# Packed attention with routed experts on Trainium2: the expert guess from VectorE's row sums, and one run of routing products over six PSUM banks

## The chip, the cores and the metric

One core of one Trainium2 chip runs the whole program in one launch. The metric is the device time of one execution in microseconds (us), and lower is better. The profile and the trace come from one profiled execution on the chip.

## What is computed

There are 8 batches of 8 heads, 576 tokens and head size 64. In each batch and head a set of 32 packed queries `p` attends over keys and values, which gives 32 packed rows. Each token's query then attends over these 32 rows, which are both its keys and its values. The 8 heads' results stand beside each other as a token row of 512 numbers, and a layer of 8 experts follows: cosine logits against 8 expert embeddings pick one expert for the token and weight its output.

```
p_packed = sm_attn(p, k, v)                  # softmax(p k^T / 8) v, 32 rows per head
x = sm_attn(q, p_packed, p_packed)           # tokens as rows of 512
xn, en = x / (|x| + 1e-6), emb / (|emb| + 1e-6)
logits = xn @ en.T / tau                     # 8 experts
e = argmax(logits); gate = softmax(logits)[e]
out = gate * (relu(x @ w1[e]) @ w2[e])       # w1: 512x1024, w2: 1024x512
```

## The kernel before, in words

Everything is float32; the large products of the expert layer are split into high and low parts of the type `fp32r` and take three products each. The order of every engine's work is written out by hand: TensorE, VectorE, ScalarE and GpSimd each run their instructions in the order in which the Python generators emit them, and semaphores alone hold one back. The expert layer of batch b, `ffn` (line 953), is the frame: it yields 56 times, after each group of its matmuls, and at each yield the driver (lines 1497 to 1517) calls `step_att` once, which emits one step of `att_main` (line 1119), the attention and routing of batch b+1. For batches 2 to 7 this order is the same each time. For batch 1 the steps come from the string list `PLAN` during batch 0's expert layer.

The steps of `ffn`: 16 times `hidden` (L1004, products against G, the first layer's weights already multiplied by the packed rows), 8 steps of L1039 (the last 64 tokens' second layer), and four chunks of 128 tokens (c = 0 to 3) with 8 steps of three L1057 matmuls each. In the last chunk `w1_rows` of the next batch (L934 on TensorE, L946 on ScalarE, L947 on VectorE, which make the next G) starts as soon as that batch's `route` has finished.

PSUM has eight banks, all given out: pool `ps` has three single banks named `pf` (the expert layer's), pool `pb` two double banks named `pt`, pool `pc` one single bank named `pu`. The order around the change:

- `att1` (line 528): `pair_turn` (L501) turns the packed rows `ppx` through TensorE, VectorE copies them to `x.T` (L568), and two steps later `row_logits` (L512: four matmuls of 8 columns) multiplies them with the embeddings `enT`; `logits_out` (L521, VectorE) puts the 8 results beside each packed row in `ppx`. The generator `queries` turns one pair of heads' queries on VectorE each time it is called (`flip`, L291); `query_scores` (L270, TensorE) needs all four turned pairs.
- `guess` (line 619): a matmul of the row logits with `itaus` (1/tau everywhere, L629) sums the logits over the packed rows; the largest of the 8 sums is the expert whose weights are loaded for the whole batch (L635 to L640 on VectorE, then DMAs from GpSimd's queue).
- `route` (line 757): for each of five chunks of tokens, two groups g of four heads and two halves of the partitions, one product (L766) of 64 rows, 128 tokens and 136 columns: 128 of values, 8 of logits. `sums` squares and adds the values on ScalarE (L778, with the accumulator read behind it) and adds the logits on VectorE (L781). Batches 1 to 7 take the chunks in two runs: chunks 0 and 1 in both `pt` tiles, and after their sums chunks 2, 3 and 4. The last chunk is computed over 128 tokens, of which the upper 64 count.
- `TURNS` (line 1080) says what each of eleven steps at the end of a batch's attention emits: `r` a step of `route`, `f` a turned pair of the next batch's keys.
- After `route`, the next batch's `quarter_banks` takes both `pt` tiles and sets their edges (L319, L320 on VectorE), and `quarter_scores` (L331) writes into them.

Of the kernel before, what the change touches and what calls it, by code (L numbers as in the profile page):

```python
# [17 lines left out]
P = 128  # L18
# [9 lines left out]
def kernel(  # L28
# [91 lines left out]

    itau = cp.tile([P, 1], F32, name="itau")
    fold = cp.tile([P, 32], F32, name="fold")
    itaus = cp.tile([P, 64], F32, name="itaus")
    enT = cp.tile([P, NPR, E], F32, name="enT")

    def embeddings():
# [41 lines left out]
                pt[:, pr * E : (pr + 1) * E], en_sb[:, pr * P : (pr + 1) * P], ident[:E, :E]  # L168
            )
        yield  # L170
        nc.scalar.copy(enT.rearrange("a b c -> a (b c)"), pt[:, : NPR * E])

    class Batch:
        def __init__(self):
# [65 lines left out]
    def rows(c):  # L240
        return P if c < 4 else 64
# [11 lines left out]
    def idle(n):  # L253
        for _ in range(n):
            yield
# [253 lines left out]
    def row_logits(x, pt, gs=range(NG)):  # L509
        for g in gs:  # L510
            for pr in range(2):
# [5 lines left out]
                    stop=True,  # L517
                )

    def logits_out(x, pt):  # L520
        nc.vector.tensor_copy(x.ppx[:, :, 2 * D :], pt[:, : NG * E].rearrange("p (g e) -> p g e", g=NG))  # L521

# [5 lines left out]
    def att1(x, nat, queries=None, other=None):  # L528

        def pack(queries, other):  # L530
            pack_tiles(x)
            if not x.s1:
                quarter_banks(x)
            quarter_scores(x)
            yield
            for g in range(NG):
                quarter_max(x, g)
            yield
            yield from whole_max(x)
# [24 lines left out]
            yield  # L564
            pu = pc.tile([P, 512], F32, name="pu", tag="pu")
            for g in range(NG):
                pair_turn(x, g, pu)
            nc.vector.tensor_copy(x.T, pu[:, 0 : NG * P])  # L568
            yield from idle(2)
            pt = pc.tile([P, 512], F32, name="pu", tag="pu")  # L570
            row_logits(x, pt)
            yield
            logits_out(x, pt)
            next(queries)
            yield

        def pack_slowly():
            pack_tiles(x)
# [20 lines left out]
            yield  # L599
            pt = pc.tile([P, 512], F32, name="pu", tag="pu")  # L600
            row_logits(x, pt)
            logits_out(x, pt)
            yield

        if x.halves:
# [13 lines left out]
    def guess(x, late=0, engine=mybir.EngineType.Pool, total=None):  # L619
# [5 lines left out]
                    pt[:1, :E], total[:, n : n + 1], enT[:, n], start=(n == 0), stop=(n == NPR - 1)  # L625
                )
        else:
            for g in range(NG):
                nc.tensor.matmul(  # L629
                    pt[:64, :E], itaus, x.ppx[:, g, 2 * D :], start=(g == 0), stop=(g == NG - 1)  # L630
                )
        yield
        m8 = sm.tile([1, 8], F32, name="m8", tag="m8", bufs=1)
        idx = sm.tile([1, 8], U32, name="idx", tag="idx", bufs=1)
# [5 lines left out]
        nc.vector.tensor_scalar(  # L640
            out=x.sel, in0=ecol[:1], scalar1=gi, scalar2=None, op0=ALU.is_equal
        )
        yield from idle(late)
        x.e = nc.values_load(
            idx[0:1, 0:1], engines=[engine], min_val=0, max_val=E - 1,
# [109 lines left out]


    def route(x):
        lg = sm.tile([P, NC5, E], F32, name="lg", tag="lg")
        ss = sm.tile([P, NC5], F32, name="ss", tag="ss")
        nc.gpsimd.memset(lg[:64, 4:5, :], 0.0)  # L760
        nc.gpsimd.memset(ss[:64, 4:5], 1.0)
        def product(c, g, to):
            n = min(c * P, S - P)
            for half in range(2):
                at = slice(64 * half, 64 * half + 64)
                nc.tensor.matmul(  # L766
                    to[:, half],
                    x.at[at, g, n : n + P],
                    x.ppx[at, g],
                    start=True,  # L770
                    stop=True,
                    tile_position=(64 * half, 0),
                )

        def sums(c, pt, lgs, sss):
            r = slice(P - rows(c), P)
            scr = sb.tile([P, 2, NG, 2 * D], F32, name="scr", tag="scr")
            nc.scalar.activation(  # L778
                scr[r, :, : pt.shape[2]], pt[r, :, :, : 2 * D], AF.Square, accum_out=sss[r]
            )  # L780
            nc.vector.tensor_reduce(  # L781
                lgs[r],
# [5 lines left out]
        def units():  # L788
# [2 lines left out]
                "p h (u w) -> p h u w", u=3  # L791
            )

        if x is bat[0]:
            for c in range(NC5):
                pt = units()
                for g in range(NG):
                    product(c, g, pt[:, :, g])
                yield
                sums(c, pt[:, :, :NG], lg[:, c], ss[:, c : c + 1])  # L800
        else:
            lg4 = sm.tile([P, E], F32, name="lg4", tag="lg4", bufs=1)
            ss4 = sm.tile([P, 1], F32, name="ss4", tag="ss4", bufs=1)
            for cs in ((0, 1), (2, 3)):
                pts = [units() for _ in cs]
                for c, pt in zip(cs, pts):
                    for g in range(NG):
                        product(c, g, pt[:, :, g])
                if cs[0]:
                    for g, pt in enumerate(pts):  # L810
                        product(4, g, pt[:, :, NG])
                yield
                for c, pt in zip(cs, pts):
                    sums(c, pt[:, :, :NG], lg[:, c], ss[:, c : c + 1])
                    yield
            sums(4, pts[0][:, :, NG:], lg[:, 4], ss[:, 4:5])
            sums(4, pts[1][:, :, NG:], lg4, ss4)
            yield
            nc.vector.tensor_tensor(out=lg[64:, 4], in0=lg[64:, 4], in1=lg4[64:], op=ALU.add)
            nc.vector.tensor_tensor(out=ss[64:, 4:5], in0=ss[64:, 4:5], in1=ss4[64:], op=ALU.add)  # L820

        nc.vector.tensor_scalar_mul(lg, lg, itau)
        mx = sm.tile([P, NC5, 1], F32, name="lmx", tag="lmx")
        nc.vector.tensor_reduce(mx, lg, axis=AX.X, op=ALU.max)
        nc.vector.tensor_tensor(
# [251 lines left out]
            drain(after.w1g)  # L1077

    AHEAD = 3
    TURNS = "r", "r", "r", "f", "f", "ff", "r", "r", "r", "r", "r"  # L1080
    STF = 2

    def out_rows(b, c):
# [75 lines left out]
    def begin():  # L1159
# [161 lines left out]
        nc.vector.tensor_scalar_mul(total, pt[:, :NPR], itau)  # L1321
        both_rows(1)
        queries(0, 0, nc.scalar.copy)
        g_guess = guess(x, 0, mybir.EngineType.SP, total)
# [58 lines left out]
        nc.gpsimd.tensor_copy(itaus, itau.broadcast_to([P, 64]))  # L1383
# [144 lines left out]
    with tc.If(n_rest > 0):  # L1528
        with tc.For_i(0, B, 1) as b:
            nb = nc.values_load(rest_i[0:1, ds(b, 1)], min_val=0, max_val=S)  # L1530
            with tc.If(nb > 0):
# [2 lines left out]
                nat = lambda i: load_nat(b, i)  # L1534
                drain(keys(x, nat, pn))
                drain(att1(x, nat))
                drain(att2(x))
                drain(route(x))
                counts(x)
# [78 lines left out]
```

## Time and profile before

| | |
|---|---|
| time, median of 3 runs | 420.41 us (420.27 to 420.61) |
| profiled execution, its own time | 420.91 us |
| span of its instructions | 419.2 us, 11033 instructions |
| mean granted TensorE clock | 0.995 of full |
| TensorE matmul busy | 408.4 us (97%) |
| VectorE busy | 307.2 us (73%) |
| ScalarE busy | 202.5 us (48%) |
| GpSimd busy | 158.7 us (38%) |

PE is TensorE's matmul row, PEld its weight loads, DVE is VectorE, ACT is ScalarE, POOL is GpSimd. L512 is line 512 of the kernel. A timeline row gives the start in us from the span's start, the length of the merged group, the engine, the line, what is written and read, and how many instructions the group has; in brackets the idle time before it and what ended it.

### The profile page before, as it was taken

Reading aid. Unit: us, or ns where it says so; the run is one execution under the profiler, and the core shown is the slowest. Engines: PE = TensorE matmul, PEld = TensorE weight load, DVE = VectorE, ACT = ScalarE, POOL = GpSimd, SP = SyncE. Lnnn points to the kernel's source line nnn. Section 1 sums busy time; section 2 is a strip of 40 time slices with the busy share of each in tenths; the row PEclk is TensorE's granted clock in tenths of the full one; section 3 lists DMA queues with packets and bytes.
Section 4 is the critical chain, followed back from the end, with each engine's and each line's share of the span. In section 5 each row is a group of like instructions: output and inputs, shape, how many; then the busy total and the mean of one; then the engine's idle time right before and its main releaser. Section 6 shows DMA issues by size and latency. Waiting matters only on the chain.

```text
span 419.2 us, 11033 instructions
## 1 busy us (share of the span) xinstructions
PE 408.4 (97%) x4036; PEld 327.9 (78%) x4037; DVE 307.2 (73%) x941; ACT 202.5 (48%) x473; POOL 158.7 (38%) x197
## 2 busy tenths in 40 slices
PE   7899999999999999999999999999999999999993
PEld 4758677697878978698777978789786987779783
DVE  3677696588977889769886889778897798566500
ACT  4577705762365714754146622656146631576110
POOL 2345714437204561336414381136613273142200
PEclk9999999999999999999999999999999999999998
DMA  8999896977999479886999669886899819310012
GB/s 225 331 338 236 220 296 221 229 189 187 298 298 235 116 216 294 284 201 172 267 316 228 169 172 280 301 216 177 225 317 262 195 39 344 121 48 5 20 48 54
DMA packets 42607, 87.93 MB, mean 210 GB/s; under 512 B 11690, under 2 KB 20906, under 8 KB 42546
## 3 DMA queue, kind: packets, MB, share of 16 engines
q1 hardware_dynamic: 35280, 61.44, 54.2%
q0 software_dynamic: 6720, 25.17, 18.4%
q8 instruction: 34, 0.56, 0.6%
q10 hardware_dynamic: 546, 0.54, 0.6%
q14 instruction: 27, 0.22, 0.2%
HBM read 77.68 MB, written 9.44 MB: 208 GB/s over the span
## 4 chain that ended last, share of the span: by engine, by line
PE 91%; DMA 4%; ACT 1%; DVE 1%; POOL 1%; SPq 0%; issue 0%; ACTq 0%; POOLq 0%
PE pf L1057 43%; PE pf L1004 24%; PE pf L1039 7%; PE pt L766 5%; DMA nat<-in_k 4%; PE pt L934 3%; PE pt L396 2%; PE pt L270 2%; PE pt L331 2%; PE pt L1233 1%; PE pu L501 0%; DMA out<-o 0%; PE pt L477 0%; PE pu L512 0%; ACT st L689 0%; PE pt L464 0%
## 5 line engine op out<-in xcount | busy, mean ns | idle before, releaser
L1057 PE MATMUL pf<-w2s,hT 128*128 128x512 f32 (+1 forms) x792 | 183.9, 388 | 0.0
L1057 PEld LDWEIGHTS pf<-w2s,hT 128*128 128x128 f32 x792 | 143.1, 188 | 39.3 <-issue 9.4
L910 POOL TENSOR_TENSOR w2s<-w2r,w2s 128x512 fp32r<-128x512 f32 x64 | 81.2, 1285 | 86.1 <-ACT w2s L909 85.3
L1004 PE MATMUL pf<-AT,G 128*128 128x288 f32 x720 | 102.1, 298 | 0.4 <-DVE hT L1009 0.2
L1004 PEld LDWEIGHTS pf<-AT,G 128*128 128x128 f32 x720 | 97.2, 188 | 4.3 <-issue 1.5
L1009 DVE SCALAR_TENSOR_TENSOR hT<-pf,hT 128x224 fp32r<-128x224 f32 (+1 forms) x128 | 52.2, 413 | 30.3 <-ACT hT L1008 29.9
L1008 ACT ACTIVATE hT<-pf 128x224 fp32r<-128x224 f32 (+1 forms) x128 | 49.3, 386 | 42.8 <-PE pf L1004 40.1
L1406 ACT ACTIVATE o<-pf,gate 128x512 f32<-128x512 f32 (+1 forms) x41 | 26.0, 635 | 32.2 <-PE pf L1057 21.2
L909 ACT CAST w2s<-w2r 128x512 fp32r<-128x512 f32 x64 | 38.7, 618 | 0.2
L291 DVE STREAM_TRANSPOSE kt<-nat 128x576 f32<-128x576 f32 x52 | 38.1, 759 | 0.0
L778 ACT ACTIVATE scr<-pt 128x512 f32<-128x512 f32 (+2 forms) x47 | 25.0, 532 | 18.0 <-PE pt L766 17.0
L1039 PE MATMUL pf<-w2r,h 128*64 128x256 f32 x256 | 33.3, 388 | 0.0
L715 POOL TENSOR_TENSOR AT<-at,AT 128x576 fp32r<-128x576 f32 x7 | 9.9, 1411 | 49.1 <-ACT AT L710 49.1
L383 POOL TENSOR_TENSOR qs<-p 128x320 f32<-128x320 f32 x12 | 10.6, 881 | 45.4 <-ACT p L364 45.4
L689 ACT ACTIVATE st<-st 128x576 f32<-128x576 f32 (+1 forms) x17 | 11.1, 657 | 33.8 <-DVE st L686 32.6
L872 ACT ACTIVATE lg<-lg 128x40 f32<-128x40 f32 x8 | 1.9, 237 | 48.4 <-DVE lg L868 48.4
L781 DVE TENSOR_REDUCE lg<-pt 128x8 f32<-128x32 f32 (+2 forms) x47 | 8.7, 185 | 22.0 <-ACT scr L778 21.7
L766 PEld LDWEIGHTS pt<-ppx,at 64*128 64x128 f32 x320 | 19.7, 186 | 6.2 <-issue 3.6
L1039 PEld LDWEIGHTS pf<-w2r,h 128*64 128x64 f32 x256 | 19.4, 137 | 4.9 <-PE pu L501 1.0
L766 PE MATMUL pt<-ppx,at 64*128 64x136 f32 x320 | 23.1, 287 | 0.0
L710 ACT CAST AT<-at 128x576 fp32r<-128x576 f32 x15 | 10.1, 675 | 22.6 <-DVE at L704 22.5
L364 ACT ACTIVATE p<-pt,qnm 128x160 f32<-128x160 f32 x48 | 17.8, 398 | 0.0
(213 smaller groups left out, 474.9 us busy)
## 6 DMA issues: line engine op xcount, KB each, us to landing
nat<-in_q SPq DMA_DIRECT2D x112, 140.0 KB, 3.5
nat<-in_k SPq DMA_DIRECT2D x96, 140.0 KB, 4.0
w1t<-in_moe_w POOLq DMA_DIRECT2D x12, 1024.0 KB, 9.3
w2r<-in_moe_w POOLq DMA_DIRECT2D x24, 512.0 KB, 16.0
out<-o SPq DMA_DIRECT2D x124, 64.0 KB, 2.1
w2r<-in_moe_w SPq DMA_DIRECT2D x8, 512.0 KB, 10.3
vn<-in_v SPq DMA_DIRECT2D x24, 160.0 KB, 3.8
vn<-in_v SPq DMA_DIRECT2D x48, 80.0 KB, 3.9
```

The source lines that it names most:

```text
L291: nc.vector.transpose(kt.rearrange("p (c i) -> p c i", i=32), t)
L364: nc.scalar.activation(x.p1[g][:, n * QW : n * QW + QW], area(x, g)[:, n // 2, n % 2], AF.Exp, bias=x.nm[:, at : at + 1],)
L766: nc.tensor.matmul(to[:, half], x.at[at, g, n : n + P], x.ppx[at, g], start=True, stop=True, tile_position=(64 * half, 0),)
L778: nc.scalar.activation(scr[r, :, : pt.shape[2]], pt[r, :, :, : 2 * D], AF.Square, accum_out=sss[r])
L909: nc.scalar.copy(t[:, 0], raw)
L910: nc.gpsimd.tensor_tensor(out=t[:, 1], in0=raw, in1=t[:, 0].bitcast(F32), op=ALU.subtract)
L1004: nc.tensor.matmul(pf[:, :HS], w, r, start=(n == 0), stop=(n == len(ops) - 1))
L1008: nc.scalar.activation(hT[:, 0, f, cs], pf[:, :n], AF.Relu)
L1009: nc.vector.scalar_tensor_tensor(out=hT[:, 1, f, cs], in0=pf[:, :n], scalar=0.0, in1=hT[:, 0, f, cs].bitcast(F32), op0=ALU.max, op1=ALU.su ...
L1039: nc.tensor.matmul(pf[64 * hf : 64 * hf + 64, :256], h4[:, f], x.w2r[f // 2][:, f % 2, hf * 256 : hf * 256 + 256], start=(f == 0), stop=(f ...
L1057: nc.tensor.matmul(pf[:, :w], hT[:, a, f, c * P : (c + 1) * P], x.w2s[f][:, m, at : at + w], start=(f == 0 and i == 0), stop=(f == NF - 1 ...
L1406: nc.scalar.activation(o[:, :w], pf[:, :w], AF.Copy, scale=x.gate[:, c : c + 1])
```

## The change

- `enT` is multiplied by 1/tau when it is made, so the multiplication by `itau` in `route` (L822) is dropped. `itaus` becomes a tile of ones, `equal`.
- `whole_rows`, new, follows the copy to `x.T`: three VectorE instructions add the 64 columns of each head pair (256 numbers to 4), multiply `enT` by the sums (32 numbers) and add over the four pairs (8 numbers).
- `row_logits` moves from `att1` into `guess`, where one matmul of `equal` with the 8 numbers takes the place of the two with `itaus`. `logits_out` moves behind the choice of the expert, ahead of the fourth query pair.
- `route` of batches 1 to 7 does all its products in one run, at the step where the second run was. The six banks are both `pt` tiles, `pu` and one `pf`. The last chunk is computed over its 64 tokens only, in four products, one for each quarter of the array. There are eight `sums` after it where there were six, then four small VectorE additions and copies where there were two.
- For batch 1 (`pack_slowly`) one yield is dropped.

```diff
+    def whole_rows(x):
+        total = sm.tile([P, NPR], F32, name="total", tag="total", bufs=1)
+        nc.vector.tensor_reduce(
+            total, x.T.rearrange("p (n j) -> p n j", n=NPR), axis=AX.X, op=ALU.add
+        )
+        part = sm.tile([P, NPR, E], F32, name="part", tag="pbd", bufs=1)
+        nc.vector.tensor_tensor(
+            out=part, in0=enT, in1=total.unsqueeze(2).broadcast_to([P, NPR, E]), op=ALU.mult
+        )
+        x.part = sm.tile([P, E], F32, name="parts", tag="parts", bufs=1)
+        nc.vector.tensor_reduce(
+            x.part, part.rearrange("p n e -> p e n"), axis=AX.X, op=ALU.add
+        )
...
             nc.vector.tensor_copy(x.T, pu[:, 0 : NG * P])
+            whole_rows(x)
             yield from idle(2)
-            pt = pc.tile([P, 512], F32, name="pu", tag="pu")
-            row_logits(x, pt)
-            yield
-            logits_out(x, pt)
             next(queries)
-            yield
+            yield from idle(2)
...
-            for g in range(NG):
-                nc.tensor.matmul(
-                    pt[:64, :E], itaus, x.ppx[:, g, 2 * D :], start=(g == 0), stop=(g == NG - 1)
-                )
+            row_logits(x, pt[:, E:])
+            nc.tensor.matmul(pt[:64, :E], equal, x.part, start=True, stop=True)
...
+        if total is None:
+            logits_out(x, pt[:, E:])
         yield from idle(late)
...
-            for cs in ((0, 1), (2, 3)):
-                pts = [units() for _ in cs]
...
+            pts = [units() for _ in range(2)]
+            ones_of = [
+                pool.tile([P, 512], F32, name=name, tag=name)[:, : 3 * XW].rearrange(
+                    "p (u w) -> p u w", u=3
+                )
+                for pool, name in ((pc, "pu"), (ps, "pf"))
+            ]
+            banks = [[pts[0][:, h], pts[1][:, h], ones_of[h]] for h in range(2)]
+            for c, spots in enumerate((
+                ((0, 0), (0, 1)), ((1, 0), (1, 1)), ((0, 2), (1, 2)), ((2, 0), (2, 1)),
+            )):
+                for g, (n, u) in enumerate(spots):
+                    for half, at in enumerate(halves):
+                        product(at, g, half, banks[half][n][:, u], slice(c * P, c * P + P))
+            for g in range(NG):
+                for half, at in enumerate(halves):
+                    product(
+                        at, g, half, ones_of[half][halves[g], 2], slice(4 * P, S), 64 * g
+                    )
+            yield
+            part = sm.tile([P, 6, E + 1], F32, name="part", tag="pbd", bufs=1)
+            lgx, ssx, every = part[:, :, :E], part[:, :, E], slice(0, P)
+            for n in range(2):
+                sums(every, pts[n][:, :, :NG], lg[:, n], ss[:, n : n + 1])
+                sums(every, pts[n][:, :, NG:], lgx[:, n], ssx[:, n : n + 1])
                 yield
+            for lo, us in ((2, slice(0, NG)), (4, slice(NG, 3))):
+                for n, t in enumerate(ones_of):
+                    sums(every, t[:, us].unsqueeze(1), lgx[:, lo + n], ssx[:, lo + n : lo + n + 1])
+                yield
+            pair = part.rearrange("p (c n) e -> p c n e", n=2)
+            nc.vector.tensor_tensor(
+                out=both[:, 2:4], in0=pair[:, :2, 0], in1=pair[:, :2, 1], op=ALU.add
+            )
+            one, two = part[:, 4], part[:, 5]
+            nc.vector.tensor_tensor(out=one, in0=one, in1=two, op=ALU.add)
+            nc.vector.tensor_copy(two[rest], one[:64])
+            nc.vector.tensor_tensor(out=both[rest, 4], in0=one[rest], in1=two[rest], op=ALU.add)
-        nc.vector.tensor_scalar_mul(lg, lg, itau)
...
-    TURNS = "r", "r", "r", "f", "f", "ff", "r", "r", "r", "r", "r"
+    TURNS = "", "", "", "f", "ff", "f", "r", "r", "r", "r", "rr"
```

## Rows read from the trace of the kernel before

**Rows 1.** The page: busy time by engine, and the chain that ended last.

```profile
PE 408.4 (97%) x4036; PEld 327.9 (78%) x4037; DVE 307.2 (73%) x941; ACT 202.5 (48%) x473; POOL 158.7 (38%) x197
PE 91%; DMA 4%; ACT 1%; DVE 1%; POOL 1%; SPq 0%; issue 0%; ACTq 0%; POOLq 0%
```

**Rows 2.** Timeline of PE, 100 to 160 us: batch 1's second layer, batch 2's routing.

```profile
102.97 11.85 PE L1057 MATMUL pf<-w2s,hT 128*128 128x512 f32 x51
114.76 1.20 PE L766 MATMUL pt<-ppx,at 64*128 64x136 f32 x16
115.89 4.42 PE L1057 MATMUL pf<-w2s,hT 128*128 128x512 f32 x18
120.23 1.66 PE L766 MATMUL pt<-ppx,at 64*128 64x136 f32 x24
121.82 3.01 PE L1057 MATMUL pf<-w2s,hT 128*128 128x512 f32 x12
...
131.06 1.26 PE L331 MATMUL pt<-kt,pw 64*32 64x160 f32 x64
...
147.38 0.35 PE L512 MATMUL pu<-enT,T 128*64 128x8 f32 x8
...
150.53 1.20 PE L270 MATMUL pt<-kt,T 64*32 64x288 f32 x32
```

**Rows 3.** Timeline of DVE, 143 to 152 us: from the turned rows to the queries.

```profile
146.85 0.41 DVE L568 COPY T<-pu 128x256 f32<-128x256 f32 x1
...
147.48 0.21 DVE L1014 TENSOR_SCALAR h<-pf 128x64 f32<-128x64 f32 x1
147.79 0.17 DVE L521 COPY ppx<-pu 128x16 f32<-128x16 f32 x1
147.96 0.78 DVE L291 STREAM_TRANSPOSE kt<-nat 128x576 f32<-128x576 f32 x1
148.87 0.16 DVE L635 MAX8 m<-pu 1x8 f32<-1x8 f32 x1
...
149.68 0.78 DVE L291 STREAM_TRANSPOSE kt<-nat 128x576 f32<-128x576 f32 x1
```

**Rows 4.** Groups by line, whole span: busy us, mean ns of one, idle before.

```profile
L680 DVE TENSOR_REDUCE mx<-st 128x18 f32<-128x576 f32 (+1 forms) x17 | 12.1, 713 | 0.5
L868 DVE TENSOR_TENSOR lg<-lg,gy 128x40 f32<-128x40 f32 x8 | 1.6, 200 | 0.3
L824 DVE TENSOR_REDUCE lmx<-lg 128x5 f32<-128x40 f32 x8 | 1.6, 197 | 0.3
```

**Rows 5.** Timeline of POOL, 145 to 150 us.

```profile
145.70 3.76 POOL L910 TENSOR_TENSOR w2s<-w2r,w2s 128x512 fp32r<-128x512 f32 x3 [1.16 <-ACT w2s L909]
```

**Rows 6.** Timeline of ACT, 112 to 136 us: the sums behind the second run.

```profile
121.77 0.60 ACT L778 ACTIVATE scr<-pt 128x512 f32<-128x512 f32 x1 [2.30 <-PE pt L766]
...
123.21 0.38 ACT L778 ACTIVATE scr<-pt 64x256 f32<-64x256 f32 x1
...
124.33 0.62 ACT L909 CAST w2s<-w2r 128x512 fp32r<-128x512 f32 x1
```

**Rows 7.** Timeline of DVE, 112 to 136 us: from the last sum to the memsets.

```profile
124.34 0.18 DVE L781 TENSOR_REDUCE lg<-pt 64x8 f32<-64x16 f32 x1 [0.33 <-ACT scr L778]
...
125.33 1.03 DVE L825 TENSOR_TENSOR lg<-lg,lmx 128x40 f32<-128x40 f32 x1
...
127.11 2.36 DVE L947 TENSOR_TENSOR G<-pt,G 128x1024 fp32r<-128x1024 f32 x2
129.56 0.11 DVE L319 MEMSET pt<- 64x64 f32 x1
...
129.94 0.11 DVE L319 MEMSET pt<- 64x64 f32 x1
```

**Rows 8.** Timeline of POOL, 112 to 136 us.

```profile
125.03 1.28 POOL L910 TENSOR_TENSOR w2s<-w2r,w2s 128x512 fp32r<-128x512 f32 x1 [9.51 <-ACT w2s L909]
```

**Rows 9.** Waits: who waited for whom, us in total, times, longest.

```profile
DVE lg L781 <- ACT scr L778: 21.7, 38, 3.4
```

More of the change, by code (lines that the diff above doesn't have):

```diff
@@ L122 @@
     fold = cp.tile([P, 32], F32, name="fold")
-    itaus = cp.tile([P, 64], F32, name="itaus")
+    equal = cp.tile([P, 64], F32, name="equal")
     enT = cp.tile([P, NPR, E], F32, name="enT")
@@ L170, in embeddings @@
         yield
-        nc.scalar.copy(enT.rearrange("a b c -> a (b c)"), pt[:, : NPR * E])
+        nc.scalar.mul(enT.rearrange("a b c -> a (b c)"), pt[:, : NPR * E], itau)
     class Batch:
@@ L598, in pack_slowly @@
             nc.vector.tensor_copy(x.T, pu[:, 0 : NG * P])
[L599 to L602, printed above, removed]
+            whole_rows(x)
             yield
@@ L757, in route, with product, sums @@
     def route(x):
-        lg = sm.tile([P, NC5, E], F32, name="lg", tag="lg")
-        ss = sm.tile([P, NC5], F32, name="ss", tag="ss")
+        both = sm.tile([P, NC5, E + 1], F32, name="lg", tag="lg")
+        lg, ss = both[:, :, :E], both[:, :, E]
         nc.gpsimd.memset(lg[:64, 4:5, :], 0.0)
         nc.gpsimd.memset(ss[:64, 4:5], 1.0)
[L762 to L776, printed above, removed]
+        def product(at, g, half, to, tokens, column=0):
+            nc.tensor.matmul(
+                to,
+                x.at[at, g, tokens],
+                x.ppx[at, g],
+                start=True,
+                stop=True,
+                tile_position=(64 * half, column),
+            )
+        def sums(r, pt, lgs, sss):
             scr = sb.tile([P, 2, NG, 2 * D], F32, name="scr", tag="scr")
+            to = scr.rearrange("p h g w -> p (h g w)")[r, : pt.shape[1] * pt.shape[2] * 2 * D]
             nc.scalar.activation(
-                scr[r, :, : pt.shape[2]], pt[r, :, :, : 2 * D], AF.Square, accum_out=sss[r]
+                to.rearrange("p (h g w) -> p h g w", h=pt.shape[1], g=pt.shape[2]),
+                pt[r, :, :, : 2 * D], AF.Square, accum_out=sss[r],
             )
@@ L792, in units @@
             )
+        rest = slice(64, P)
+        halves = [slice(64 * half, 64 * half + 64) for half in range(2)]
         if x is bat[0]:
@@ L796, in route @@
                 pt = units()
+                n = min(c * P, S - P)
                 for g in range(NG):
-                    product(c, g, pt[:, :, g])
+                    for half, at in enumerate(halves):
+                        product(at, g, half, pt[:, half, g], slice(n, n + P))
                 yield
-                sums(c, pt[:, :, :NG], lg[:, c], ss[:, c : c + 1])
+                sums(slice(P - rows(c), P), pt[:, :, :NG], lg[:, c], ss[:, c : c + 1])
         else:
-            lg4 = sm.tile([P, E], F32, name="lg4", tag="lg4", bufs=1)
@@ L803, in route @@
-            ss4 = sm.tile([P, 1], F32, name="ss4", tag="ss4", bufs=1)
-            for cs in ((0, 1), (2, 3)):
-                pts = [units() for _ in cs]
[L806 to L811, printed above, removed]
-                yield
-                for c, pt in zip(cs, pts):
-                    sums(c, pt[:, :, :NG], lg[:, c], ss[:, c : c + 1])
-                    yield
@@ L816, in route @@
[L816 to L820, printed above, removed]
-        nc.vector.tensor_scalar_mul(lg, lg, itau)
+            pts = [units() for _ in range(2)]
[5 more added lines that the diff above has]
+            ]
@@ new lines, in route @@
+            banks = [[pts[0][:, h], pts[1][:, h], ones_of[h]] for h in range(2)]
[6 more added lines that the diff above has]
+            for g in range(NG):
+                for half, at in enumerate(halves):
+                    product(
+                        at, g, half, ones_of[half][halves[g], 2], slice(4 * P, S), 64 * g
+                    )
@@ L1320, in begin @@
         total = sm.tile([P, NPR], F32, name="total", tag="total", bufs=1)
-        nc.vector.tensor_scalar_mul(total, pt[:, :NPR], itau)
+        nc.vector.tensor_copy(total, pt[:, :NPR])
         both_rows(1)
@@ L1382, in begin @@
             yield
-        nc.gpsimd.tensor_copy(itaus, itau.broadcast_to([P, 64]))
+        nc.gpsimd.memset(equal, 1.0)
         nc.vector.tensor_reduce(
@@ L1536 @@
                 drain(att1(x, nat))
+                pt = pc.tile([P, 512], F32, name="pu", tag="pu")
+                row_logits(x, pt)
+                logits_out(x, pt)
                 drain(att2(x))
```

1 line of the change is left out of this document (added).

## The prediction, made before the change was run

> **What bounds the kernel now.** I read the page first: TensorE is busy for 97% of the span and holds 91% of the chain that ended last [rows 1]. So a microsecond taken from TensorE's queue is a microsecond of the kernel, as long as TensorE then does not wait for somebody. VectorE at 73% looks free, but that is an average; whether it is free where the change puts work is the question. Second, the timeline of TensorE over one batch [rows 2]: it shows the order of its groups, where both routing runs (L766) lie, and where TensorE next needs VectorE: at the query scores (L270) and at the next batch's key scores (L331). Third, the timelines of VectorE, ScalarE and GpSimd ahead of these two places [rows 3, 5 to 8]. I work on the stretch of batch 2's routing and batch 3's attention and count it for every batch whose steps are emitted in the same order.
>
> **TensorE's gain in routing.** The pace of the L1057 matmuls where nothing breaks in is (114.76 - 102.97) / 51 = 0.231 us [rows 2]. The first run takes TensorE from 114.76 to 115.89, 1.13 us, the second from 120.23 to 121.82, 1.59. The 8 further records of the second cost 0.46, or 0.115 a pair (two halves run side by side). The matmuls behind a run also restart slowly: 18 take 4.34 where the pace gives 4.16, and 12 some 0.17 too long. So both runs cost 2.72 + 0.35 = 3.07 us; 20 pairs are 2.31, and each run's edges 0.38. After the change there are 16 pairs (1.85), one pair of edges (0.38), and the last chunk. Its four products in four quarters of the array are in no row; bounds: two steps of 0.115 where all four run side by side (0.23), or four steps and another 0.2 for the turn to the smaller tile (0.66). I take 0.34, nearer the first, since the halves do run side by side. That is 2.57 against 3.07: 0.5 saved (0.2 to 0.6), for seven batches **3.5 us** (1.4 to 4.2).
>
> **VectorE's added work before the query scores.** This is the first price. In [rows 3] VectorE runs from the copy of the turned rows (146.85) to the end of the fourth query pair (149.68 + 0.78 = 150.46) with two short idle spots, 0.1 between L1014 and L521 and 0.13 between the third pair and L635. TensorE starts L270 at 150.53 [rows 2], which leaves that pair 0.07 us. `whole_rows` puts three instructions right behind the copy. The sum of 256 numbers: between 40 numbers (0.197) and 576 (0.713) [rows 4] a straight line gives 0.40. The product of 32: 0.20, as L868's 40. The sum of 32: 0.19, as L824. With some 0.03 between dependent ones that is 0.9 us. The two idle spots take up at most 0.23 of it. L521 moves behind the choice of the expert and stays ahead of the fourth pair, so its move wins nothing. The least that the pair moves is about 0.65 us.
>
> One thing may add to it. The product reads two SBUF tensors at about 147.7, while GpSimd runs three L910 one behind the other from 145.70 to 149.46, 1.28 us each [rows 5, 8], so the second ends near 148.2. In [rows 7, 8] L825, 40 numbers that take 0.20 as L868 does, lasts from 125.33 to 126.36 and ends just when GpSimd's L910 (125.03 to 126.31) does: it waited. By that row the product waits up to 0.4, so the pair moves by 0.65 to 1.05. I take 0.8, as the product meets the second L910 only near its end. TensorE arrives earlier by what the joining of L512 and the guess saves; at most the 0.35 of L512's group [rows 2], and I take 0.15, which the wait eats. Who is late next: L270, every matmul behind it, and the softmax with it. Against 150.53 it starts 0.8 - 0.07 later, some **0.7 us** in each of batches 2 to 7: **+4.2 us** (+3.4 to +6). Batch 1 has its queries turned long before; I count nothing, since its row sums lie two steps ahead of the guess's matmul.
>
> **ScalarE's chain behind the run.** This is the second price. Count from the start of the run. Before, ScalarE's first sum starts at 121.77 - 120.23 = 1.54, when the first `pt` tile's last product is written; that is the tenth pair, and so it is after the change. The four sums of before then take 2.56 us, to L909 at 124.33 [rows 6]: 0.72 for one of 512 numbers, 0.5 to 0.6 for one of 256. After the change there are eight: 2 x 0.72, 4 x 0.55 and 2 x 0.45 (128 numbers, an estimate from the other two sizes) = 4.5, with one L909 (0.62) among them. The last VectorE sum, which ended at 124.52 or 4.3, ends at 1.54 + 4.5 + 0.6 + 0.2 = 6.9 us.
>
> Every sum on VectorE waits for ScalarE's on the same bank, 38 times in this trace [rows 9]; no row shows ScalarE coming back to a tile that VectorE has just read, which the change does twice, so it costs 0 to 2 x 0.23 (the sum's 0.19 and its signal). I take 0.3: 7.2 us. The Trainium skill (PSUM — Partial Sum Buffer, PSUM bank collisions raise a hardware error) says that ScalarE and VectorE may not read one bank's quarter at the same time, so a program must keep them in turn; no run yet shows the second direction. By that rule it is the full 0.46 and the sum below is 0.8 us more over five batches; without it, 1.5 us less.
>
> Behind the last sum VectorE has a chain without a gap: small steps of `route`, L825, both L947 of the next G, the memsets. From 124.52 to the second bank's memset at 129.94 it is 5.4 us [rows 7], and L331 starts at 131.06, so it had some 1.1 us to spare. After the change four small steps instead of three and the missing scaling (L822) come out at +0.15, and the first of them, with two SBUF inputs, may meet the L910 that follows the earlier L909 (0 to 0.3). The chain ends at 7.2 + 5.4 + 0.3 = 12.9. TensorE reaches L331 9.24 us after the run (131.06 - 121.82), and the run takes about 2.4 from its start: 11.6. So L331 waits some **1.2 us**. Ends: nothing, if L825 runs free of GpSimd (0.83 less) and the tiles cost no turns; 1.9 where all add up. It falls behind the routing of batches 2 to 6. In batch 1's L825 is free and the route one step earlier, I count 0; batch 7's has no L331 behind it, only the first L1004 of its layer, which needs the first G: 0.3. In all 5 x 1.2 + 0.3 = **+6.3 us** (0 to +10).
>
> **Priced at nothing.** The dropped L822, the memset of `equal`, and the scaling in the start run on engines with idle time there. The run's other two banks: `pf` was freed by a store two chunks back, `pu` by the guess 25 us before. The last sums free that `pf` for the second L1004 group, some 4 us later. The weights' DMAs start about 0.7 us later behind the guess, with over 20 us to their use. The keys' four turns come up to 0.7 us earlier.
>
> **The sum.** -3.5 + 4.2 + 6.3 = +7.0 us against the profiled execution's own 420.91, so 427.9. Its span is 419.2, the rest lies around it; the median of the runs shown is 0.5 lower, so the prediction is **427.4 us**.
>
> **Rivals.** A difference of 0.2% (0.84 us) is about what a measurement can tell.
> - *Only the query scores wait* (15%): ScalarE's eight sums run at 0.45 each, L825 meets no L910, and the chain ends before 11.6. Then -3.5 + 4.2: 421.1 us, and with the lower end of the query price (+3.4) 420.3. For it: 1.1 us of slack before. Against it: four more sums are 2 us by the rows.
> - *Both waits fit, faster* (15%). The place is VectorE between L568 and the fourth pair: if the three added instructions take at most 0.07 us beyond its idle spots, and L331 finds its banks at 11.6, TensorE keeps its 3.5 and 0.15 of each of six joined guesses: 416.0 us. It decides at the 0.07 us of [rows 3]: any instruction that does not fit an idle spot is lost one to one. Against it: the sum of 256 alone is 0.4.
> - *The quarters do not run side by side, and all turns add up* (15%): the gain is 1.4, L331 waits 1.9: -1.4 + 6 + 9.8 = +14.4, 434.8 us.
> - My forecast, both waits: 55%.
>
> **The numbers.** The range is 417.5 to 432: it takes in the first rival and the forecast with its bounds, and leaves out the better half of the second and the worse half of the third. Faster by over 0.2%: the second rival and a little of the first, 0.17. Within: most of the first, 0.1. Slower: the rest, 0.73.
>
> **What would show it.** Right: L270's weight loads idle some 0.7 us for VectorE's L291 in batches 2 to 7; L331's idle about 1.2 us for the memsets; one L766 group of 40 records of about 2.4 us; the added product stretched to the end of an L910. Wrong: L270 a few hundredths behind L629's group with no idle time, or L331 at its old distance from the run; then VectorE or ScalarE had room that I did not see.

## The result, and the profile after

The changed kernel takes **423.97 us** (median of 6 runs) where the kernel before takes 420.79 on the same chip: a ratio of 1.0077 (95% interval 1.0056 to 1.0097). One of its six runs took 430.77 us at a lower granted clock, and the ratio leaves it out. The kernel is slower, as forecast, and inside the range, but by about 3 us and not by 7. The span of the profiled execution is 422.2 us against 419.2. In the changed file L766 is now L773 (the products), L778 and L781 are L785 and L789 (the sums on ScalarE and VectorE), L1057 is L1088, L1004 is L1035, L910 is L941, L825 is L856, L629 is L638; `whole_rows` is L523, L527 and L531, and the four small steps behind the sums are L846, L850, L851 and L852.

The page of the changed kernel: busy time, and the chain that ended last.

```profile
PE 409.5 (97%) x4022; PEld 327.6 (78%) x4023; DVE 311.8 (74%) x982; ACT 202.9 (48%) x501; POOL 158.6 (38%) x197
PE 86%; DVE 5%; ACT 3%; DMA 2%; issue 1%; POOL 1%; SPq 0%; DVEq 0%; ACTq 0%; POOLq 0%
```

Against [rows 1] the busy times hardly tell anything. The chain does: TensorE's share fell from 91% to 86%, and VectorE and ScalarE, which had 1% each, now hold 8% between them. There are places where TensorE waits for them. Timeline of PE in the changed kernel:

```profile
46.63 0.44 PE L501 MATMUL pu<-ident,ppx 128*128 128x128 f32 x2
...
71.42 2.36 PE L1088 MATMUL pf<-w2s,hT 128*128 128x512 f32 x9
75.76 0.92 PE L1088 MATMUL pf<-w2s,hT 128*128 128x512 f32 x3 [1.98 <-DVE lg L846]
...
99.36 0.38 PE L501 MATMUL pu<-ident,ppx 128*128 128x128 f32 x2
...
103.75 1.79 PE L270 MATMUL pt<-kt,T 64*32 64x288 f32 x32
105.47 15.93 PE L1088 MATMUL pf<-w2s,hT 128*128 128x512 f32 x69
121.33 1.66 PE L773 MATMUL pt<-ppx,at 64*128 64x136 f32 x24
...
123.17 0.28 PE L773 MATMUL pu<-ppx,at 64*128 64x136 f32 x1
...
123.39 0.33 PE L773 MATMUL pu<-ppx,at 64*64 64x136 f32 x1
...
123.55 0.28 PE L773 MATMUL pu<-ppx,at 64*64 64x136 f32 x1
...
123.78 3.04 PE L1088 MATMUL pf<-w2s,hT 128*128 128x512 f32 x12
...
132.16 0.95 PE L1035 MATMUL pf<-AT,G 128*128 128x288 f32 x6
133.18 1.25 PE L331 MATMUL pt<-kt,pw 64*32 64x160 f32 x64
...
148.25 0.38 PE L501 MATMUL pu<-ident,ppx 128*128 128x128 f32 x2
...
152.65 1.78 PE L270 MATMUL pt<-kt,T 64*32 64x288 f32 x32
```

The kernel before at the same places, the rows that stand with [rows 2]:

```profile
46.79 0.44 PE L501 MATMUL pu<-ident,ppx 128*128 128x128 f32 x2
...
97.47 0.38 PE L501 MATMUL pu<-ident,ppx 128*128 128x128 f32 x2
...
130.18 0.95 PE L1004 MATMUL pf<-AT,G 128*128 128x288 f32 x6
...
146.16 0.38 PE L501 MATMUL pu<-ident,ppx 128*128 128x128 f32 x2
```

Four things are to be read here, with the turn of the packed rows (L501) as the mark of each batch.

- **The query scores.** From L501 to the start of the second layer: 105.47 - 99.36 = 6.11 us, before 102.97 - 97.47 = 5.50. L270 starts as long after the turn as before (4.39 against 4.37), but lasts 1.79 where it lasted 1.20 [rows 2]: the part of it that needs the fourth pair comes late. That is 0.61 lost, in each of batches 2 to 7.
- **Routing.** From the start of the second layer to the matmuls behind the last product: 123.78 - 105.47 = 18.31, before 121.82 - 102.97 = 18.85 [rows 2]. That is 0.54 won. The quarters of the array run side by side: the last chunk's records start in two groups, 123.39 and 123.55.
- **The key scores.** From the first group of L1035 to L331: 133.18 - 132.16 = 1.02, before 131.06 - 130.18 = 0.88. That is 0.14 lost.
- **One wait of 1.98 us**, once, in batch 0's second layer, that no step of the prediction has.

From L501 to L501 a batch takes 48.89 where it took 48.69. The first such stretch, with the wait in it, takes 99.36 - 46.63 = 52.73 where it took 97.47 - 46.79 = 50.68.

The waits of the changed kernel: who waited for whom, us in total, times, longest.

```profile
ACT scr L785 <- DVE lg L789: 3.8, 14, 0.5
PEld pt L270 <- DVE kt L291: 2.7, 6, 0.5
PE pf L1088 <- DVE lg L846: 2.0, 1, 2.0
```

Timelines of VectorE and of GpSimd from the turned rows to the queries, which answer to [rows 3, 5]; the first line is the turn of the next batch's keys, ahead of routing:

```profile
120.87 2.75 DVE L291 STREAM_TRANSPOSE kt<-nat 128x576 f32<-128x576 f32 x4
...
148.94 0.41 DVE L583 COPY T<-pu 128x256 f32<-128x256 f32 x1
149.38 0.42 DVE L523 TENSOR_REDUCE total<-T 128x4 f32<-128x256 f32 x1
149.84 0.53 DVE L527 TENSOR_TENSOR part<-enT,total 128x32 f32<-128x32 f32 x1
150.40 0.20 DVE L531 TENSOR_REDUCE parts<-part 128x8 f32<-128x32 f32 x1
...
152.46 0.76 DVE L291 STREAM_TRANSPOSE kt<-nat 128x576 f32<-128x576 f32 x1
```
```profile
147.79 3.76 POOL L941 TENSOR_TENSOR w2s<-w2r,w2s 128x512 fp32r<-128x512 f32 x3 [1.16 <-ACT w2s L940]
```

The fourth pair starts 152.46 - 148.94 = 3.52 behind the copy to `x.T`, where it started 149.68 - 146.85 = 2.83 behind it [rows 3]. The sum of 256 numbers took 0.42 and the last sum 0.20. The product took 0.53 instead of the 0.19 that it takes in batch 1, where GpSimd is idle: it ends at 150.37, when the second of GpSimd's three L941 does (147.79 and two thirds of 3.76 is 150.30).

Timelines of ScalarE, VectorE and GpSimd behind the run, which answer to [rows 6 to 8]:

```profile
122.87 0.60 ACT L785 ACTIVATE scr<-pt 128x512 f32<-128x512 f32 x1 [2.12 <-PE pt L773]
...
123.81 0.39 ACT L785 ACTIVATE scr<-pt 128x256 f32<-128x256 f32 x1 [0.26 <-DVE lg L789]
```
```profile
127.97 0.17 DVE L789 TENSOR_REDUCE part<-pf 128x8 f32<-128x8 f32 x1 [0.23 <-ACT scr L785]
128.06 0.61 DVE L846 TENSOR_TENSOR lg<-part 128x18 f32<-128x18 f32 x1
...
129.48 0.20 DVE L856 TENSOR_TENSOR lg<-lg,lmx 128x40 f32<-128x40 f32 x1
...
132.92 0.11 DVE L320 MEMSET pt<- 64x64 f32 x1
133.12 0.11 DVE L319 MEMSET pt<- 64x64 f32 x1
```
```profile
127.35 1.28 POOL L941 TENSOR_TENSOR w2s<-w2r,w2s 128x512 fp32r<-128x512 f32 x1 [9.25 <-ACT w2s L940]
```

The last sum ends at 128.14, 6.81 us behind the start of the run. L846 lasts 0.61 and ends with GpSimd's L941 at 128.6; in batch 1, where GpSimd is idle there, it takes 0.17. L856 then takes 0.20, where L825 took 1.03 [rows 7]: GpSimd runs one instruction in this stretch, and it holds up one VectorE instruction, not two. L331 starts 0.15 after the first bank's memsets (132.92 + 0.11) have ended.

### The profile page after: what moved, and what is told of

Same layout as the page of the kernel before. It is cut to its first block, busy times and chain, and to the rows that moved or that the text cites. A ratio compares the mean times of both kernels' runs of the same rounds, so it can differ in the third digit from the quotient of the medians.

```text
span 422.2 us, 11085 instructions
## 1 busy us (share of the span) xinstructions
PE 409.5 (97%) x4022; PEld 327.6 (78%) x4023; DVE 311.8 (74%) x982; ACT 202.9 (48%) x501; POOL 158.6 (38%) x197
## 4 chain that ended last, share of the span: by engine, by line
PE 86%; DVE 5%; ACT 3%; DMA 2%; issue 1%; POOL 1%; SPq 0%; DVEq 0%; ACTq 0%; POOLq 0%
PE pf L1088 38%; PE pf L1035 24%; PE pf L1070 7%; PE pt L965 3%; PE pt L773 3%; PE pt L270 2%; PE pt L396 2%; PE pt L331 2%; PE pu L773 1%; DMA out<-o 1%; PE pf L1232 1%; DMA nat<-in_k 1%; ACT scr L785 1%; PE pt L464 1%; DVE kt L291 1%
## 5 line engine op out<-in xcount | busy, mean ns | idle before, releaser
L1088 PE MATMUL pf<-w2s,hT 128*128 128x512 f32 (+1 forms) x792 | 182.0, 387 | 2.0 <-DVE lg L846 2.0
L1088 PEld LDWEIGHTS pf<-w2s,hT 128*128 128x128 f32 x792 | 143.6, 188 | 41.3 <-issue 13.1
L941 POOL TENSOR_TENSOR w2s<-w2r,w2s 128x512 fp32r<-128x512 f32 x64 | 80.9, 1285 | 84.8 <-ACT w2s L940 82.7
L1035 PE MATMUL pf<-AT,G 128*128 128x288 f32 x720 | 102.1, 298 | 0.4 <-DVE hT L1040 0.2
L1035 PEld LDWEIGHTS pf<-AT,G 128*128 128x128 f32 x720 | 97.2, 188 | 4.3 <-issue 1.5
L1040 DVE SCALAR_TENSOR_TENSOR hT<-pf,hT 128x224 fp32r<-128x224 f32 (+1 forms) x128 | 52.3, 414 | 24.2 <-ACT hT L1039 23.7
L785 ACT ACTIVATE scr<-pt 128x512 f32<-128x512 f32 (+2 forms) x33 | 16.8, 508 | 19.7 <-PE pt L773 15.6
L978 DVE TENSOR_TENSOR G<-pt,G 128x1024 fp32r<-128x1024 f32 x14 | 16.5, 1218 | 1.7 <-ACT G L977 1.7
L930 POOL DMA_DIRECT2D w2r<-in_moe_w x24 | 17.0, 713 | 0.0
L773 PEld LDWEIGHTS pt<-ppx,at 64*128 64x128 f32 x208 | 12.7, 186 | 3.7 <-issue 2.5
```

Source lines behind the costliest of these rows:

```text
L773: nc.tensor.matmul(to, x.at[at, g, tokens], x.ppx[at, g], start=True, stop=True, tile_position=(64 * half, column),)
L785: nc.scalar.activation(to.rearrange("p (h g w) -> p h g w", h=pt.shape[1], g=pt.shape[2]), pt[r, :, :, : 2 * D], AF.Square, accum_out=sss[r],)
L941: nc.gpsimd.tensor_tensor(out=t[:, 1], in0=raw, in1=t[:, 0].bitcast(F32), op=ALU.subtract)
L1035: nc.tensor.matmul(pf[:, :HS], w, r, start=(n == 0), stop=(n == len(ops) - 1))
L1040: nc.vector.scalar_tensor_tensor(out=hT[:, 1, f, cs], in0=pf[:, :n], scalar=0.0, in1=hT[:, 0, f, cs].bitcast(F32), op0=ALU.max, op1=ALU.su ...
L1088: nc.tensor.matmul(pf[:, :w], hT[:, a, f, c * P : (c + 1) * P], x.w2s[f][:, m, at : at + w], start=(f == 0 and i == 0), stop=(f == NF - 1 ...
```

## The experiments

All edits are against the changed kernel. A run's ratio is against the kernel before on the same chip; a "stretch" is the time from one L501 to the next in its trace. The theory that these rows suggest: the loss has two causes, the late fourth pair (0.61 in six batches) and the one wait for a `pf` bank; the one run of products is a gain by itself. The rival, from the prediction: the eight sums keep L331 waiting, so that the routing loses.

### The guess as before, routing as changed

```diff
-            whole_rows(x)
             yield from idle(2)
+            pt = pc.tile([P, 512], F32, name="pu", tag="pu")
+            row_logits(x, pt)
+            yield
+            logits_out(x, pt)
             next(queries)
-            yield from idle(2)
+            yield
...
-            row_logits(x, pt[:, E:])
-            nc.tensor.matmul(pt[:64, :E], equal, x.part, start=True, stop=True)
+            for g in range(NG):
+                nc.tensor.matmul(
+                    pt[:64, :E], equal, x.ppx[:, g, 2 * D :], start=(g == 0), stop=(g == NG - 1)
+                )
...
```

> The one run of products over six banks as in the change, the guess as before (row logits two steps after the turned rows, two matmuls for the guess, no row sums on VectorE). Theory: routing itself gains 0.54 us in each of seven batches, loses some 2 us once, in batch 0's layer, where TensorE waits for a bank that batch 1's sums hold, and 0.13 in five batches ahead of the key scores: -3.8 + 2.0 + 0.7 = about -1.1 us against before, 419.6. In the trace L270 starts its two parts together, as before. Rival, that the eight sums behind the run are what costs: 422 or more, with the wait still there ahead of L331 or L1035.

422.11 us, 1.0012 (0.9997 to 1.0028). The stretches of batches 2 to 6 are 48.28, 0.41 less than before, and L270 doesn't wait, as expected. The total missed by 2.5 us: the first stretch is 54.43, 3.75 longer than before. The wait for a `pf` bank is there too, and longer, since batch 1's steps aren't one earlier as in the change. The rest is TensorE's clock. Timeline of PE, and the granted clock in the page's 40 slices of 10.5 us:

```profile
76.26 2.90 PE L1094 MATMUL pf<-w2s,hT 128*128 128x512 f32 x6 [2.46 <-DVE lg L852]
PEclk9999999899999999999999999999999999999998
```

The first 8 is the slice from 73.6 to 84.1 us. Behind the idle 2.46 us the granted clock is 0.50 from 77 to 79 us, the lower of its two levels (1.2 GHz and not 2.4), and 1.00 again from 80. From the end of the wait to the next L501, with the same matmuls, this kernel takes 25.16 us, and the changed kernel, whose clock stays at 1.00 in its trace, 23.60. So the slower clock cost 1.56 us here. The 2.2 that are left of the 3.75 are the price of the bank, less what batch 1's routing gains. The run alone didn't settle what the wait costs, so the next ones take the two causes apart.

### The guess as changed, routing as before

```diff
+        elif True:
...
+            for cs in ((0, 1), (2, 3)):
+                pts = [units() for _ in cs]
...
-            for turn in TURNS:
+            for turn in (("r", "r", "r", "f", "f", "ff", "r", "r", "r", "r", "r") if True else ("", "", "", "f", "ff", "f", "r", "r", "r", "r", "rr")):
```

> The guess from VectorE's row sums as in the change, routing in two runs as before in all batches. Theory: the second part of the query scores L270 waits some 0.6 us for the fourth query pair in each of batches 2 to 7 and nothing is gained: +3.6 us against before, 424.4. Rival, that the guess is free because VectorE has idle time: within 0.5 us of before, with the whole loss of the change in routing.

424.48 us, 1.0071 (1.0054 to 1.0087). Timeline of PE in this kernel:

```profile
146.46 0.38 PE L501 MATMUL pu<-ident,ppx 128*128 128x128 f32 x2
...
195.77 0.38 PE L501 MATMUL pu<-ident,ppx 128*128 128x128 f32 x2
```

A stretch is 49.31, 0.62 above the kernel before, and the two-run routing takes its old time. The guess alone costs as much as the whole change.

### Batch 1 alone in two runs

```diff
+        elif x is bat[1]:
...
+            for cs in ((0, 1), (2, 3)):
+                pts = [units() for _ in cs]
...
-            for turn in TURNS:
+            for turn in (("r", "r", "r", "f", "f", "ff", "r", "r", "r", "r", "r") if x is bat[1] else ("", "", "", "f", "ff", "f", "r", "r", "r", "r", "rr")):
```

> The changed kernel, but batch 1 alone routes in two runs as before. Theory: TensorE's one wait of 1.98 us in the last chunk of batch 0's layer goes, batch 1's gain of 0.54 goes too: 1.4 us faster than the changed kernel, 422.5. Rival, that this wait only moves (to the first layer's weights or the key scores of batch 2): no faster than 423.7.

422.46 us, 1.0026 (1.001 to 1.0042). The wait of 1.98 us is gone, the first stretch is 50.99 and the others 48.89 as in the change. The wait belongs to batch 1's route.

### The sums that hold the bank, first

Why only there? In `ffn` the store of a chunk is emitted inside the next one, by `if f == STF and len(last) > late`. In batch 0's layer `late` is true, and each store comes one chunk later. When the fourth chunk asks for a bank, two of the three `pf` banks hold chunks that aren't stored, and the third holds the route's products until the last of eight sums has read it. Timeline of VectorE in the changed kernel, batch 1:

```profile
75.45 0.17 DVE L789 TENSOR_REDUCE part<-pf 128x8 f32<-128x8 f32 x1 [0.23 <-ACT scr L785]
75.53 0.17 DVE L846 TENSOR_TENSOR lg<-part 128x18 f32<-128x18 f32 x1
```

That sum ends at 75.62 and the matmuls go on at 75.76. The name L846 in the wait is that of the instruction behind it. If that is the cause, another order of batch 1's sums is enough, with the one run kept. It was tried on both versions of the guess.

```diff
+            if x is bat[1]:
...
+                pair(0, 0)
+                one(1, 0)
+                one(1, 1)
                 yield
...
+                pair(0, 1)
+                pair(1, 0)
+                pair(1, 1)
...
```

`pair` and `one` make the same sums, of a `pt` bank pair and of a single bank; `one(1, ...)` are the two of the `pf` bank. On the changed kernel:

> The changed kernel with the same new order of batch 1's sums. Theory: the wait of 1.98 us in batch 0's last chunk goes, nothing else changes: 1.8 us faster than the changed kernel, 422.1. Rival: the wait moves, 424.

422.12 us, 1.0017 (1.0006 to 1.0029), and the first stretch is 50.52: against 52.73 the wait and its restart cost 2.21 us. With the guess as before:

> The guess as before, all seven batches in one run, and in batch 1 alone the two sums of the bank from the pool pf come second and third of the eight instead of sixth and eighth. Theory, that batch 0's last chunk waits for this one bank: it is free about 3 us earlier, the wait of 2.5 us that the same kernel had with the old order falls to under 0.5, and batch 1 gains what the other batches gain: 418 us, 2.5 to 2.9 below before. Rival, that the wait moves to the products of the first weights (L934 of before) or that it comes from the run as such: 421 or more, as with the old order.

418.26 us, 0.9921 (0.9903 to 0.9939): faster than the kernel before and than the changed one. Its timelines of VectorE and of PE:

```profile
73.08 0.17 DVE L795 TENSOR_REDUCE part<-pf 128x8 f32<-128x8 f32 x1 [0.43 <-ACT scr L791]
```
```profile
71.78 3.25 PE L1123 MATMUL pf<-w2s,hT 128*128 128x512 f32 x12
```

The bank is free at 73.25, and the 12 matmuls behind the run are one group again. They take 3.25 us where the same order of sums on the changed kernel has 3.04, so some 0.2 us of the wait is left.

### Routing without the guess, and without batch 1

The edits of the first and the third experiment together.

> The guess as before; one run of products for batches 2 to 7, and batch 1 in two runs as before. Theory: the routing's gain of 0.41 us a batch stands alone, five full periods and the last half: 2.5 us faster than before, 418.2, with no period of batch 1 changed. Rival, that the missing wait of batch 1 comes back elsewhere or the gain is lost to VectorE: within 0.8 us of before.

418.45 us, 0.993 (0.9912 to 0.9947), which can't be told from the 0.9921 of the kernel above. Timeline of PE:

```profile
145.67 0.38 PE L501 MATMUL pu<-ident,ppx 128*128 128x128 f32 x2
...
193.97 0.38 PE L501 MATMUL pu<-ident,ppx 128*128 128x128 f32 x2
```

48.30 a batch: one run of products is worth 0.4 us in each, though ScalarE makes eight sums instead of six. The rival falls.

### The fourth pair ahead of the guess

Can the row sums be kept and their price avoided? Here the fourth query pair is turned before the choice of the expert, so that L270 needn't wait for both.

```diff
             whole_rows(x)
             yield from idle(2)
             next(queries)
-            yield from idle(2)
+            yield
+            next(queries)
+            yield
...
-                if n == 1 and queries:
-                    next(queries)
```

> The changed kernel, but the fourth query pair is turned one step after the third, ahead of the choice of the expert on VectorE instead of behind it; the same instructions otherwise. Theory: the pair ends some 0.8 us earlier, the wait inside L270 goes, and each of batches 2 to 7 gains 0.5 to 0.6 us: 3 us faster than the changed kernel, 421. Rival, that L270's second part waits for something else than VectorE's order (the guess, a load, TensorE's own switch): same as the changed kernel, 424.

424.14 us, 1.0058 (1.0036 to 1.0079): the expectation missed by 3 us. The wait at L270 went, and another came. Waits in this kernel, then the timelines of PE and of VectorE ahead of it:

```profile
PEld pt L331 <- PE pf L1037: 3.8, 5, 0.8
PE pt L331 <- DVE pt L320: 2.8, 5, 0.6
```
```profile
122.85 1.66 PE L775 MATMUL pt<-ppx,at 64*128 64x136 f32 x24
```
```profile
122.97 2.75 DVE L291 STREAM_TRANSPOSE kt<-nat 128x576 f32<-128x576 f32 x4
125.64 0.15 DVE L791 TENSOR_REDUCE lg<-pt 128x8 f32<-128x32 f32 x1
```

TensorE comes to the run 0.6 earlier, VectorE doesn't. The turned keys ahead of the first sum end 2.9 us into the run (2.3 in the change: 120.87 + 2.75 against 121.33), so the chain of sums starts later and L331 waits 0.5 to 0.6 for the memsets. Nearly all that L270 gained went there: a stretch is 48.80. Another 1.6 us of its trace is in the first stretch (54.36), and it is the clock again, as in the first experiment:

```profile
PEclk9999999899999999999999999999999999999999
```

Behind an idle time of 2.04 us for the `pf` bank the granted clock is 0.50 from 77 to 80 us, and from the wait's end to the next L501 it takes 25.23 us against 23.60.

The new theory: from the turned rows to L331's memsets VectorE has no time left over, and a reordering within it only moves the wait. To test it, 0.76 us of its work ahead of the run went to GpSimd (the subtraction that makes the low part of half of `AT`), with batch 1 in two runs and the early pair, and the same kernel was run without that move.

```diff
-        second = att2(x, flips, b == 0, b < 1, ENG1 if b == 1 else "vvvvpv")
+        second = att2(x, flips, b == 0, b < 1, ENG1 if b == 1 else "vvvvpp")
```

Without the move:

> The changed kernel with batch 1 in two runs and the fourth query pair ahead of the choice of the expert. Theory, that VectorE's own time from the turned rows to the memsets is what binds: the 0.6 us that leave L270 come back ahead of L331, as they did with the query pair alone; about 0.5 us faster than with batch 1's two runs alone, 422. Rival, that the two waits are independent: 419.

421.86 us, 1.0003 (0.999 to 1.0016); L331 waits 3.0 us in five places, a stretch is 48.80. With it:

> As the one before, and the subtraction for the low part of the second half of the attention weights (0.76 us a batch on VectorE, just ahead of the keys' four turns) goes to GpSimd in batches 2 to 7. Theory, VectorE's backlog binds: the keys' turns end 0.68 us earlier, so the first sum on VectorE does not come late, the wait ahead of L331 goes, the period falls from 48.8 to 48.3: 3 us faster than the one before, 419. Rival, that ScalarE's eight sums in a row bind: as the one before, 422.

419.28 us, 0.9945 (0.9925 to 0.9965), a stretch 48.29. Timelines of PE and of VectorE:

```profile
119.01 1.66 PE L775 MATMUL pt<-ppx,at 64*128 64x136 f32 x24
...
130.84 1.25 PE L331 MATMUL pt<-kt,pw 64*32 64x160 f32 x64
```
```profile
118.06 2.71 DVE L291 STREAM_TRANSPOSE kt<-nat 128x576 f32<-128x576 f32 x4
121.27 0.19 DVE L791 TENSOR_REDUCE lg<-pt 128x8 f32<-128x32 f32 x1 [0.50 <-ACT scr L787]
```

Now the keys end 1.8 into the run, the first sum waits for ScalarE and not for VectorE, and L331 starts 11.83 behind the start of the run (133.18 - 121.33 = 11.85 in the change, 135.18 - 122.85 = 12.33 with the early pair alone). That shows the theory for this order of the steps. It also shows that the row sums, once paid for, win nothing: 48.29 is what the old guess has with one run of products.

Last, the same move with the old guess, to see whether the 0.14 us ahead of L331 goes too:

> The guess as before, one run of products for batches 2 to 7, and the same subtraction on GpSimd. Theory: only the 0.13 us ahead of L331 are left to win in each of five batches: 0.6 us faster than without the move, 417.6. Rival, that GpSimd's subtraction holds up a VectorE step with two SBUF inputs or a weight split: slower than without the move.

419.47 us, 0.9948 (0.993 to 0.9965), no gain over 418.45 and a stretch of 48.28 as there. The expectation missed: the keys are done early enough that VectorE's first sum waits 1.11 us for ScalarE's, and L331 still starts 11.83 us behind the run in both kernels. So that 0.14 hangs on the chain from ScalarE's first sum on, and not on the turned keys. The 1.0 us more in the total is not in the stretches: in this trace the first L501 comes at 48.55 and not at 46.70, and with the same move on the new guess it comes at 46.49. Why it is late is open.

## Why the prediction was right on the side and wrong on the size

| step | predicted | measured |
|---|---|---|
| one run of products | -3.5 | 0.54 in six batches, 0.4 in batch 1: -3.6 |
| L270 behind the fourth pair | 0.7 x 6 = +4.2 | 0.61 x 6 = +3.7 |
| L331 behind the sums | 1.2 x 5 + 0.3 = +6.3 | 0.14 x 5 = +0.7 |
| batch 1's guess | 0 | +0.3 |
| the `pf` bank in batch 0's layer | 0 | +2.2 |
| sum | +7.0 | +3.3 |

The spans differ by 3.0; the 0.3 between is the rounding of the terms and a start that came 0.16 earlier (46.63 against 46.79).

**Right: the run.** 2.45 us from 121.33 to 123.78. In batch 1 the gain is read between experiments with the new guess and without the wait: first stretches of 50.94 and 50.99 with two runs and 50.52 with one. With the old guess it is 0.26 (50.69 and 50.43), less by the 0.2 that was left of the wait there. The four quarters ran side by side; they and the turn to the smaller tile (0.22 from 123.17 to 123.39, where a pair has 0.115) cost about 0.4, priced at 0.34.

**Right, with some luck: the row sums.** The sum, the product and the last sum were priced at 0.9 without GpSimd; alone they would be 0.82, and GpSimd's block added 0.33, within the 0 to 0.4. The pair moved by 0.69 (taken: 0.8). Two errors cancel in that. Up to the first instruction behind the row sums VectorE lost 1.25 (the next L1040 starts 1.58 behind the copy, L1009 before the change 0.33), more than the 0.9 and the 0.15 for GpSimd that were taken. But it caught up 0.56 of it, and not the 0.23 of the two idle spots. One reason is that L521's move did win something: it took 0.17, with 0.1 idle ahead of it, and at its new place it costs 0.08. The 0.15 of the joined guess didn't come: L270 starts 4.39 behind the turn, as before. It wouldn't have counted, as the prediction says.

**Wrong: "The chain ends at 7.2 + 5.4 + 0.3 = 12.9".** In the same terms, to the second bank's memset, it ended at 133.12 - 121.33 = 11.8. The step that failed is the 5.4 + 0.3. It kept L825's stretched 1.03 from [rows 7], and its 0.3 is 0.15 for the four small steps and as much again for GpSimd ahead of it, but the same single L941 stood behind both waits. Once L846 had waited for it, L856 ran free, and this part took 4.98. The sums were 0.4 shorter as well (6.81 for 7.2). TensorE came at 11.7 (11.6 predicted), so a term of 1.2 became 0.14. The lower end of the term held it, but the likeliest value didn't.

Within the sums, the two turns between ScalarE and VectorE on one bank cost 0.26 each, 0.52 together: the upper end, where 0.3 was taken. The program keeps the two engines in turn on the bank, and ScalarE pays for it, 14 times in all. The Trainium skill (PSUM — Partial Sum Buffer, PSUM bank collisions raise a hardware error) says that two engines may not access one quadrant of a bank at once, two reads included. The trace agrees, in that ScalarE waits 0.26 us and then starts when VectorE has read. The sums and the cast among them, priced at 4.5 + 0.6, took 4.55 without the turns, which more than made up.

**Wrong: "`pf` was freed by a store two chunks back", priced at nothing.** That is so in the layers of batches 1 to 6, and was read in batch 1's layer. In batch 0's layer the stores lag by a chunk, and the bank that the run takes is missing: 2.2 us, and some 1.6 more where the clock falls behind it. The kernel's own condition, `len(last) > late`, says it; the prediction took one layer for all.

**Wrong, small: batch 1's guess at 0.** The row sums stand two steps ahead there, but VectorE still came too late. Timeline of PE in the changed kernel:

```profile
50.74 0.19 PE L638 MATMUL pu<-parts,equal 128*64 128x8 f32 x1 [0.28 <-DVE lg L789]
```

The signs of the steps came out as forecast, with two errors that partly cancelled: 5.6 too much at L331, 2.2 missing at `pf`. So that the kernel is slower by a clear margin is in large part luck. What the prediction's own three steps turned out to be worth adds up to +0.8, no more than it said a measurement can tell. The other 2.5 stand where it put nothing. The changed kernel without the wait agrees: 422.12 us, 0.8 above before. At L331 the first rival (15%) came nearer than the forecast: only the query scores wait by much, and L856 meets no L941, as that rival asks. No rival had the `pf` bank.

One reading priced at nothing is off without effect: `pu` was freed by the guess some 20 us before the run, and not 25.

## What to carry to other kernels

An engine that is 26% idle over the span can have no time at all between two points of the schedule; then moving an instruction within that stretch moves the wait, and what removed it here was taking work away from the engine. One block by another engine must be counted once: when an earlier instruction meets it, the one that met it before runs free. Where a step borrows a buffer of another loop, look for the one pass in which that loop holds its buffers longer. When one stretch of a trace is longer than its waits say, read the granted clock there.

## What was not expected of the hardware

Three L941 stand back to back on GpSimd, from 147.79 to 151.55, and yet VectorE's product got in at 150.37, behind the second; it didn't wait for the third. L846 as well ended with the one L941 that was running. In both the wait is as long as what was left of one GpSimd instruction. The Trainium skill (SBUF — State Buffer, Who interferes with whom) says that a VectorE instruction with two SBUF inputs and a GpSimd instruction that reads SBUF exclude each other, by a lock that is held for the whole instruction. The 0.53 and 0.61 us here for work of about 0.2 agree.

A wait of TensorE can cost more than its length. After 2.46 and 2.04 us without work the granted clock stood at 0.50 for about 3 us, which cost some 1.6 us more each time; after 1.98 us in the changed kernel's trace it stayed at 1.00. Why it fell in two traces and not in the third, these runs don't show.
